# r's exponentials in place in PSUM, zero products in TensorE's first waits, casts behind the second pair's products, two weight quarters earlier, and two chunks' transposes on TensorE

## The chip, the cores and the metric

The kernel runs on one core of one Trainium2 chip. The metric is the device time of one execution in microseconds (us). Engines are named as in the profile: PE is TensorE's matmul, PEld its weight load, DVE is VectorE, ACT is ScalarE, POOL is GpSimd, SP is SyncE, which here issues nearly all DMAs.

## The reference

Two stages. The first is a linear attention with a decay per channel (4 batches, 8 heads, 768 positions, 48 channels per head), the second a feed-forward product with a leaky ReLU on its 3072 x 384 output:

```python
for t in range(S):
    cur = np.einsum('bhd,bhe->bhde', u[None] * kt, vt)
    y[:, :, t] = np.einsum('bhd,bhde->bhe', rt, state + cur)
    state = wt[:, :, :, None] * state + np.einsum('bhd,bhe->bhde', kt, vt)
x = y.transpose(0, 2, 1, 3).reshape(B * S, H * D)
h = x @ w_in                      # 384 -> 2048
out = np.maximum(0.01 * h, h) @ w_out   # 2048 -> 384
```

All inputs and the output are float32.

## The kernel before, in words

**Tiling.** The 3072 rows are 24 chunks of 128 positions, 6 for each batch. A chunk's attention gives y (128 x 384), which is transposed into columns of xT. Its feed-forward part is 4 up groups (12 matmuls each, xT by a quarter of w_in, line 821), a leaky ReLU by ACT (line 855), and 4 down groups (4 matmuls of 384 columns each, line 873) that add into one PSUM bank; the result is copied and stored. Chunks 0 and 1, and 2 and 3, are worked on together as a pair (`pair`, lines 491 to 666), the rest one by one (`single`, lines 668 to 794).

**Attention of a chunk.** ACT takes the logarithm of w into lw (line 332). PE sums it along the positions into the bank cp (`cum`, lines 521 and 691). The decay factors are exponentials of these sums (`grow`, line 342): er for r and ek for k. A single takes er from cp, and ek from ci = cp + lw, which DVE computes (line 716). A pair needs four: er[1] and ek[0] from cp, er[0] and ek[1] from two other sums, which for both pairs PE computes into two more banks (lines 543 and 544). DVE multiplies r by er and k by ek into rk (`product`, line 348). rk is transposed into rkT (`turn`): by four PE transposes for each of r and k (line 391), with copies out of PSUM by DVE (line 399) and ACT (line 401), or from chunk 12 on by one DMA transpose (line 382). Scores are products of rkT (lines 629 and 750), masked by DVE (line 412). The state goes from chunk to chunk: outer products of k and v (lines 594 and 761), added by DVE to the shrunken old state (line 434); POOL does the shrinking (line 421). y is the sum of products in bank yp (lines 646, 654, 780, 785) and of a diagonal term vs that POOL and DVE prepare (lines 357 to 371); DVE adds them (line 444). Then y is transposed by PE (line 458) and copied by ACT (line 465), from chunk 12 on by DMA (line 450). The a exponentials (lines 569 and 738) read cp as well.

**Order.** Nothing is ordered by hand. Each step is added to `Plan` with its engine, a cost in us and a priority; `Plan.order` runs a small model of the engines (line 71: PE costs count 1.8 times before 26 us of the model's time; lines 76 to 81: DMA) and the instructions are issued in the order of the model's start times. Each engine works through its instructions in that order. Attention of chunk n has priority 10n or 10n + 1 (smaller goes first), casts of the weights 3 (`CASTS`), feed-forward products 1000 and more. PE's instructions of all chunks are one queue, and so are DVE's and SP's.

**Weights.** w_in and w_out come as four quarters each (0.79 MB), loaded by SP (lines 290 and 295); each is cast to bf16, one half by DVE (line 313), the other by ACT (line 315). `WEIGHTS` says with which chunk a quarter is added and at which priority: the first with pair 2 at priority 20.15, the other seven with chunk 4 at 24. Pair 2's loads of w, k, r and v have 20.0, 20.1, 20.2 and 20.3, so the first quarter stands between k and r.

**PSUM.** Eight banks: hp and op two each, cp, yp, se and so one each. A `Ring` hands out its banks in turn; a step that writes a bank waits for all steps that used it before.

```python
PAIRS = (0, 2)
TDMA = range(12, NCH)
WEIGHTS = [(2, 20.15)] + [(4, 24.0)] * 7
CASTS = 3
```

Of the kernel before, what the change touches and what calls it, by code (L numbers as in the profile page):

```python
# [15 lines left out]
class Plan:  # L16
# [20 lines left out]
    def order(self):  # L37
# [19 lines left out]
        while events:  # L57
            now, e = heapq.heappop(events)
            if free[e] > now + 1e-9:
                continue  # L60
            while coming[e] and coming[e][0][0] <= now + 1e-9:
                _, i = heapq.heappop(coming[e])
                heapq.heappush(ready[e], (self.pri[i], i))
            if not ready[e]:
                if coming[e]:
                    heapq.heappush(events, (coming[e][0][0], e))
                continue
            _, i = heapq.heappop(ready[e])
            start[i] = now
            count += 1  # L70
            free[e] = now + self.dur[i] * (1.8 if e == "PE" and now < 26 else 1)
            if self.wire[i] is None:
                done[i] = free[e] + self.LAT[e]
            else:

                flying = [x for x in flying if x[0] > free[e]]
                while sum(x[1] for x in flying) + self.rows[i] > 3300:
                    free[e] = max(free[e], flying.pop(0)[0])
                dma_free = max(dma_free, free[e]) + self.wire[i]
                done[i] = dma_free + 1.6  # L80
                flying.append((done[i], self.rows[i]))
            heapq.heappush(events, (free[e], e))
            for j in users[i]:
                left[j] -= 1
                same = self.eng[j] == e and self.wire[i] is None
                ready_at[j] = max(ready_at[j], free[e] if same else done[i])
                if not left[j]:
                    f = self.eng[j]
                    heapq.heappush(coming[f], (ready_at[j], j))
                    heapq.heappush(events, (max(ready_at[j], free[f]), f))  # L90
# [33 lines left out]
def kernel(  # L124
# [23 lines left out]
    OACT = 14  # L148
    NCI = 3
    TDMA = range(12, NCH)  # L150
    LEAD = 8
    AHEAD = 5

    PAIRS = (0, 2)
    PWIRE, WIRE = 1.45, 1.15
    WEIGHTS = [(2, 20.15)] + [(4, 24.0)] * 7
    CASTS = 3
    blocks = [1] * NCH
# [9 lines left out]
    trev = pool.tile([128, 128], BF16, name="trev")  # L168
    trex = pool.tile([128, 128], BF16, name="trex")
    maskb = pool.tile([128, 128], BF16, name="maskb")  # L170
    pmask = pool.tile([128, 2, 128], BF16, name="pmask")
    pev = pool.tile([128, 128], BF16, name="pev")
    pex = pool.tile([128, 128], BF16, name="pex")
    halves = pool.tile([128, 2], BF16, name="halves")
    ident = pool.tile([128, 128], BF16, name="ident")
# [10 lines left out]
    ci_r = ring("ci", 2, [128, H, D], F32)  # L186
    er_r = ring("er", 3, [128, H, D], F32)
    ek_r = ring("ek", 2, [128, H, D], F32)
# [17 lines left out]
    cp_r = ring("cp", 1, [128, 512], F32, psum)  # L206
    yp_r = pp_r = ring("yp", 1, [128, 512], F32, psum)
    se_r = ring("se", 1, [128, 512], F32, psum)
    so_r = ring("so", 1, [128, 512], F32, psum)

    with tc.manual_schedule():
        nc.scalar.preload_act_table_set("natural_log_exp_and_others")

        for t, op in ((trev, ALU.is_ge), (trex, ALU.is_gt)):
            nc.gpsimd.memset(t[:], -1.0)
            nc.gpsimd.affine_select(
                out=t[:], in_=t[:], compare_op=op, fill=0.0,
                base=0, pattern=[[-1, 128]], channel_multiplier=1,
            )
# [21 lines left out]
        for q in (0, 64):  # L241
            for i, op in ((slice(0, 64), ALU.is_gt), (slice(64, 128), ALU.is_gt),
                          (slice(128, 192), ALU.is_ge), (slice(192, 256), ALU.is_gt)):
                t = pmask[q : q + 64].rearrange("p a t -> p (a t)")[:, i]
                nc.gpsimd.affine_select(
                    out=t, in_=t, compare_op=op, fill=0.0,
                    base=0, pattern=[[1, 64]], channel_multiplier=-1,
                )
        nc.vector.memset(onef[:], 1.0)
        nc.vector.memset(halves[:], 0.0)  # L250
# [34 lines left out]
        def weight_steps(q, which, pri):  # L285
# [13 lines left out]

            ld = step("SP", 0.45, load, pri, writes=[st], wire=2.0, rows=(384, 512)[which])  # L300
            made = []
# [42 lines left out]

        def product(rk, a, xn, e, P0, deps, n):
            return step(
                "DVE", 0.65 if n < 2 else 0.84 - 0.04 * a,
                lambda: nc.vector.tensor_tensor(out=rk.t[:, a, :, 0:D], in0=xn.t, in1=e.t[:], op=ALU.mult),  # L348
# [124 lines left out]
        def spread_u():  # L473
# [3 lines left out]
                -1, wire=0.05)  # L477
            up = op_r.take()
            s_ub = step(
# [11 lines left out]
        def pair(n):  # L491
# [45 lines left out]
            cums.extend([s_cum, s_cum])  # L537
            er = [er_r.take() for _ in range(2)]
            ek = [ek_r.take() for _ in range(2)]
            if n < NCI:  # L540
                cs = [(hp_r if n == 0 else op_r).take() for _ in range(2)]
                s_c = [
                    step("PE", 0.33, lambda: sums(cs[0].t, pev, pev), P0, reads=lw, writes=[cs[0]], deps=s_ln),
                    step("PE", 0.33, lambda: sums(cs[1].t, pex, pex), P0, reads=lw, writes=[cs[1]], deps=s_ln)]
                e_in = [hd(x.t[:, 0:DM]) for x in cs]
                s_w = []
            else:
                cs = [ci_r.take() for _ in range(2)]
                s_c = [
                    step(  # L550
                        "DVE", dve(DM, 120),
                        lambda j=j: nc.vector.tensor_tensor(
                            out=cs[j].t[:], in0=hd(cp.t[:, 0:DM]), in1=lw[j].t[:, :, 0:D],
                            op=(ALU.subtract, ALU.add)[j]),
                        P0, reads=[cp, lw[j]], writes=[cs[j]], deps=[s_cum])
                    for j in range(2)]
                e_in = [x.t[:] for x in cs]
                s_w = s_c
            mid = hd(cp.t[:, 0:DM])
            s_er1 = grow(er[1], cp, mid, 1.0, P0, [s_cum, *s_w])  # L560
            s_ek0 = grow(ek[0], cp, mid, -1.0, P0, [s_cum, *s_w])
            s_er0 = grow(er[0], cs[0], e_in[0], 1.0, P0, [s_c[0]])
            s_ek1 = grow(ek[1], cs[1], e_in[1], -1.0, P0, [s_c[1]])

# [12 lines left out]
            for j in range(2):  # L577
                s_k = product(rk[j], 1, kn[j], ek[j], P0, [kl, (s_ek0, s_ek1)[j]], n)
                s_r = product(rk[j], 0, rn[j], er[j], P0, [rl, (s_er0, s_er1)[j]], n)
                s_d.append([s_r, s_k])  # L580
# [5 lines left out]

            pps = [op_r.take(), op_r.take()] if n == 0 else [se_r.take(), so_r.take()]

# [79 lines left out]
        def single(n):  # L668
# [33 lines left out]
            cums.append(s_cum)  # L702
            er, ek = er_r.take(), ek_r.take()
            if n < NCI:
                cq = op_r.take()
                s_ci = step(
                    "PE", 0.17,
                    lambda: nc.tensor.matmul(
                        hd(cq.t[:, 0:DM]), lhsT=trex[:], rhs=lw.t[:, :, 0:D], start=True, stop=True),
                    P0, reads=[lw], writes=[cq], deps=[s_ln])  # L710
                ci, e_in, s_w = cq, hd(cq.t[:, 0:DM]), [s_cum]
            else:
                ci = ci_r.take()
                s_ci = step(
                    "DVE", dve(DM, 120),
                    lambda: nc.vector.tensor_tensor(  # L716
                        out=ci.t[:], in0=hd(cp.t[:, 0:DM]), in1=lw.t[:, :, 0:D], op=ALU.add),
                    P0, reads=[cp, lw], writes=[ci], deps=[s_cum, s_ln])
                e_in, s_w = ci.t[:], [s_cum, s_ci]
            s_er = grow(er, cp, hd(cp.t[:, 0:DM]), 1.0, P0, s_w)  # L720
            s_ek = grow(ek, ci, e_in, -1.0, P0, [s_ci])
            rk = rk_r.take()
            s_r = product(rk, 0, rn, er, P0, [rl, s_er], n)
            s_k = product(rk, 1, kn, ek, P0, [kl, s_ek], n)
            rkT = rkT_r.take()
# [7 lines left out]
            if not first:  # L733
# [5 lines left out]
                            out=a_in.t[q0 : q0 + 64, :, half], in_=cp.t[q0 : q0 + 64, DM : DM + NP], func=AF.Exp),  # L739
                        P0 + 1, reads=[cp], writes=[a_in], deps=s_w)  # L740
                    for half, q0 in ((0, 0), (1, 64))]
# [56 lines left out]
        while n < NCH:  # L798
# [3 lines left out]
            else:  # L802
                single(n)
                n += 1


# [90 lines left out]
        for n in range(NCH):  # L897
            if n >= LEAD:
                plan.deps[lns[n]].append(up_done[n - LEAD])
        for i in plan.order():  # L900
            plan.fn[i]()

# [29 lines left out]
```

## Time and profile before

| | us |
|---|---|
| median of 3 runs (lowest, highest) | 188.97 (188.82, 189.43) |
| the profiled execution | 188.97 |
| its span from first to last instruction | 187.3 |
| PE busy | 174.0 (93%) |
| DVE busy | 128.0 (68%) |
| ACT busy | 116.3 (62%) |
| POOL busy | 108.7 (58%) |
| first up group | 19.84 |
| last down group begins / copy of the last result | 180.44 / 183.90 |

The profile is one execution. Busy times are sums over an engine's instructions; matmuls are pipelined, so 12 matmuls that each take 0.219 us fill 0.67 us when they follow one another. In a line of the order in time the first figure is the start, the second the time covered, then engine, line of the kernel, operation, output<-input by the program's names, shape and count; in brackets how long the engine was idle before it and what released it. A group's line has busy us, mean ns of one, and the idle time before. The chain that ended last is followed back from the last instruction. "issue" is a wait for nothing that the profile shows.

### The profile page before, as it was taken

The page shows a single profiled execution, that of the slowest core. Times are in us where ns is not written, and L with a number is a line of the kernel's source. Part 1 is how long each engine was busy: PE and PEld are TensorE (multiplying, and loading weights), DVE is VectorE, ACT ScalarE, POOL GpSimd, SP SyncE. Part 2 cuts the span into 40 slices and gives each one's busy share as a digit, 9 for nine tenths or more (in the row PEclk, how much of TensorE's full clock was granted, in tenths as well). Part 3 has the DMA queues.
Part 4 walks back from the last instruction along what each step waited for, and adds up shares of the span by engine and source line. Part 5 has one row for each costly group of instructions (what it writes and reads, how often), then busy time and mean ns, then how long its engine had stood idle before and what let it go on. Part 6 is the DMA issues. An engine that isn't in the chain of part 4 may idle for free.

```text
span 187.3 us, 6219 instructions
## 1 busy us (share of the span) xinstructions
PE 174.0 (93%) x2550; PEld 136.1 (73%) x2550; DVE 128.0 (68%) x226; ACT 116.3 (62%) x254; POOL 108.7 (58%) x148
## 2 busy tenths in 40 slices
PE   3678579999999999999999999999999999999992
PEld 1255567688778878788787787878887877877871
DVE  2399784887789787877967999766876856441111
ACT  2646586678876877796687666676374645334430
POOL 7799922175899898978792885170545755400000
PEclk9999999999999999999999999999999999999999
DMA  5999999889899997987899879997789996512102
GB/s 147 261 316 322 385 370 302 156 189 217 164 221 211 185 221 158 221 193 172 174 207 190 156 155 229 119 200 141 159 180 179 191 202 142 123 44 67 38 7 84
DMA packets 116383, 34.62 MB, mean 185 GB/s; under 512 B 109697, under 2 KB 114818, under 8 KB 116354
## 3 DMA queue, kind: packets, MB, share of 16 engines
q1 hardware_dynamic: 116352, 34.22, 82.9%
q8 instruction: 20, 0.33, 0.7%
q14 instruction: 9, 0.07, 0.1%
q10 hardware_dynamic: 2, 0.00, 0.0%
HBM read 25.17 MB, written 4.72 MB: 160 GB/s over the span
## 4 chain that ended last, share of the span: by engine, by line
PE 81%; SPq 7%; DMA 6%; issue 1%; POOL 1%; DVE 1%; POOLq 0%; DVEq 0%
PE op L873 33%; PE hp L821 32%; DMA in<-in_moe_w_out_dram 6%; SPq L470 4%; PE se L750 3%; SPq L290 3%; PE yp L785 2%; PE cp L691 2%; PE yp L761 2%; PE yp L780 1%; PE so L391 1%; PE se L391 1%; PE yp L458 1%; PE cp L696 1%; PE yp L654 1%
## 5 line engine op out<-in xcount | busy, mean ns | idle before, releaser
L855 ACT ACTIVATE g<-hp 128x512 bf16<-128x512 f32 x96 | 57.1, 597 | 42.3 <-PE hp L821 41.4
L821 PE MATMUL hp<-xT,w_in_b 128*128 128x128 bf16 x1152 | 79.0, 219 | 0.3 <-DVE rkT L399 0.3
L873 PE MATMUL op<-w_out_b,g 128*128 128x384 bf16 x384 | 76.5, 326 | 0.8 <-DVE w_out_b L313 0.8
L821 PEld LDWEIGHTS <-w_in_b 128*128 128x128 bf16 x1152 | 69.3, 98 | 7.2 <-DVE w_in_b L313 0.2
L873 PEld LDWEIGHTS <-g 128*128 128x128 bf16 x384 | 33.0, 97 | 15.6 <-issue 0.9
L357 POOL TENSOR_TENSOR ru<-in,ub 128x384 f32<-128x384 f32 x24 | 26.9, 1119 | 19.7 <-DMA in<-in_r_dram 19.7
L369 POOL TENSOR_TENSOR vs<-in,dg 128x384 f32<-128x384 f32 x24 | 20.2, 843 | 14.7 <-DVE dg L365 11.0
L361 POOL TENSOR_TENSOR ru<-ru,in 128x384 f32<-128x384 f32 x24 | 25.7, 1072 | 0.9
L348 DVE TENSOR_TENSOR rk<-in,er 128x384 bf16<-128x384 f32 x24 | 18.2, 757 | 7.4 <-DMA in<-in_r_dram 5.5
L348 DVE TENSOR_TENSOR rk<-in,ek 128x384 bf16<-128x384 f32 x24 | 22.0, 919 | 1.4 <-ACT a L738 0.9
L421 POOL TENSOR_TENSOR sb<-s,a 128x384 bf16<-128x384 f32 x17 | 16.1, 947 | 10.7 <-DVE s L434 10.1
L412 DVE TENSOR_TENSOR m<-se,maskb 128x512 bf16<-128x512 f32 x20 | 13.8, 689 | 7.3 <-PE so L750 7.1
L444 DVE TENSOR_TENSOR y<-yp,vs 128x384 bf16<-128x384 f32 x24 | 13.3, 553 | 7.5 <-PE yp L785 5.1
L889 DVE COPY o<-op 128x384 f32<-128x384 f32 x10 | 5.6, 558 | 18.2 <-PE op L873 18.1
L337 POOL CAST vb<-in 128x384 bf16<-128x384 f32 x24 | 14.6, 614 | 4.5 <-DMA in<-in_v_dram 4.5
L332 ACT ACTIVATE lw<-in 128x384 bf16<-128x384 f32 x24 | 12.4, 520 | 3.9 <-DMA in<-in_w_dram 3.8
L365 DVE TENSOR_REDUCE dg<-ru 128x8 f32<-128x384 f32 x24 | 13.0, 543 | 1.9 <-POOL ru L361 1.8
L412 DVE TENSOR_TENSOR m<-so,maskb 128x512 bf16<-128x512 f32 x20 | 13.6, 680 | 0.0
L342 ACT ACTIVATE er<-cp 128x384 f32<-128x384 f32 x22 | 10.8, 492 | 3.5 <-DVE ci L716 3.0
L716 DVE TENSOR_TENSOR ci<-cp,lw 128x384 f32<-128x384 f32 x20 | 11.0, 549 | 1.8 <-ACT g L855 0.9
L342 ACT ACTIVATE ek<-ci 128x384 f32<-128x384 f32 x20 | 10.5, 526 | 0.0
L391 PEld LDWEIGHTS <-rk 128*128 128x128 bf16 x96 | 6.7, 103 | 5.0 <-DVE rk L348 4.2
(103 smaller groups left out, 191.0 us busy)
## 6 DMA issues: line engine op xcount, KB each, us to landing
out_dram<-o SPq DMA_DIRECT2D x24, 192.0 KB, 2.5
in<-in_w_dram SPq DMA_DIRECT2D x20, 192.0 KB, 3.6
in<-in_k_dram SPq DMA_DIRECT2D x20, 192.0 KB, 3.8
in<-in_r_dram SPq DMA_DIRECT2D x20, 192.0 KB, 3.9
in<-in_v_dram SPq DMA_DIRECT2D x20, 192.0 KB, 3.8
in<-in_moe_w_in_dram SPq DMA_DIRECT2D x4, 768.0 KB, 8.5
in<-in_moe_w_out_dram SPq DMA_DIRECT2D x4, 768.0 KB, 12.6
in<-in_w_dram SPq DMA_DIRECT2D x2, 384.0 KB, 5.0
```

Of the source, the lines that this page charges most:

```text
L337: "POOL", 0.57, lambda: nc.gpsimd.tensor_copy(out=vb.t[:], in_=vn.t),
L342: "ACT", 0.5, lambda: nc.scalar.activation(out=out.t[:], in_=i, func=AF.Exp, scale=scale),
L348: lambda: nc.vector.tensor_tensor(out=rk.t[:, a, :, 0:D], in0=xn.t, in1=e.t[:], op=ALU.mult),
L357: lambda: nc.gpsimd.tensor_tensor(out=ru.t[:], in0=rn.t, in1=ubv, op=ALU.mult),
L361: lambda: nc.gpsimd.tensor_tensor(out=ru.t[:], in0=ru.t[:], in1=kn.t, op=ALU.mult),
L369: lambda: nc.gpsimd.tensor_tensor(out=vs.t[:], in0=vn.t, in1=dg.t[:].unsqueeze(2).to_broadcast([128, H, D]), op=ALU.mult),
L412: lambda par=par: nc.vector.tensor_tensor(out=m.t[:, par], in0=gt(sc[par].t), in1=mask.unsqueeze(1).to_broadcast([128, NP, 128]), op=ALU.m ...
L421: lambda: nc.gpsimd.tensor_tensor(out=sb.t[:].rearrange("p g a d -> p (g a) d"), in0=s_in.t[:].rearrange("p g a d -> p (g a) d"), in1=a_ap ...
L444: lambda: nc.vector.tensor_tensor(out=y.t[:], in0=hd(yp.t[:, 0:DM]), in1=vs.t[:], op=ALU.add),
L821: nc.tensor.matmul(hp.t[:, a * N : (a + 1) * N], lhsT=w_in_b[:, t, (j + a) * 128 : (j + a + 1) * 128], rhs=xT[:, t, c0 : c0 + N], start=(a ...
L855: lambda hp=hp, g=g, j=j, J=J, N=N: nc.scalar.activation(out=g.t[:, j : j + J, 0:N], in_=hp.t[:, 0 : J * N].rearrange("p (a n) -> p a n", ...
L873: nc.tensor.matmul(op.t[:, 0:DM], lhsT=g.t[:, j, off : off + 128], rhs=w_out_b[:, j, :], start=(j == 0), stop=(j == NJ - 1))
```

## The change

Six things are different:

1. The exponentials er for r are written over the sums that they are made from: into cp, and for er[0] of a pair into the bank of its own sum. The buffers er are gone. ek[1] of a pair is written in place as well (a PSUM bank for pair 0, the SBUF buffer ci for pair 2). Where er and ek both come from cp, ek is computed first.
2. Pair 2 computes its second extra sum on DVE (cp + lw) and no longer on PE.
3. As long as the previous PE step ends before 24 us of the model's time, each PE step is preceded by products of a tile of zeros (256 columns each, into the second op bank): one per 0.13 us of 70% of the gap that the model leaves between the two steps. The first op bank alone (`pre_r`) serves the steps that took op banks before; pair 0's second outer product goes to the yp bank.
4. Casts of the weights have priority 21 in place of 3.
5. Two weight quarters are loaded at priority 4, behind pair 0's loads and ahead of pair 2's; the other six at 24, behind pair 2's.
6. DMA transposes begin with chunk 14, not 12. The model's constants are others: the factor 1.8 ends at 6 us and not at 26, DMA times are a few per cent longer, products count 0.58 or 0.84.

```diff
-            free[e] = now + self.dur[i] * (1.8 if e == "PE" and now < 26 else 1)
+            free[e] = now + self.dur[i] * (1.8 if e == "PE" and now < 6 else 1)
...
-    TDMA = range(12, NCH)
+    TDMA = range(14, NCH)
...
-    PWIRE, WIRE = 1.45, 1.15
-    WEIGHTS = [(2, 20.15)] + [(4, 24.0)] * 7
-    CASTS = 3
+    PWIRE, WIRE = 1.5, 1.18
+    WEIGHTS = [(2, 4.0)] * 2 + [(4, 24.0)] * 6
+    WARM = 24.0
+    CASTS = 21
...
+    pre_r = Ring(op_r.tiles[:1])
...
-            er = [er_r.take() for _ in range(2)]
-            ek = [ek_r.take() for _ in range(2)]
-            if n < NCI:
-                cs = [(hp_r if n == 0 else op_r).take() for _ in range(2)]
+            for j, banks in enumerate((hp_r, hp_r) if n == 0 else (pre_r, None)):
...
+            mid = View(cp, hd(cp.t[:, 0:DM]))
+            ek = [ek_r.take(), e_in[1]]
+            er = [e_in[0], mid]
+            s_ek0 = grow(ek[0], cp, mid.t, -1.0, P0, [s_cum, *s_w])
+            s_er1 = grow(mid, cp, mid.t, 1.0, P0, [s_cum, s_ek0, *s_w])
+            s_er0 = grow(er[0], cs[0], er[0].t[:], 1.0, P0, [s_c[0]])
+            s_ek1 = grow(ek[1], cs[1], ek[1].t[:], -1.0, P0, [s_c[1]])
...
-            pps = [op_r.take(), op_r.take()] if n == 0 else [se_r.take(), so_r.take()]
+            pps = [pre_r.take(), yp_r.take()] if n == 0 else [se_r.take(), so_r.take()]
...
+            er = View(cp, hd(cp.t[:, 0:DM]))
+            s_er = grow(er, cp, er.t, 1.0, P0, [s_cum, s_ci])
+            s_ek = grow(ek, ci, ci.t[:], -1.0, P0, [s_ci])
...
+        at = 0.8
         for i in plan.order():
+            if plan.eng[i] == "PE" and at < WARM:
+                for _ in range(int((plan.start[i] - at) * 0.7 / 0.13)):
+                    nc.tensor.matmul(
+                        op_r.tiles[1][:, 0:256], lhsT=zeros[:, 0:128], rhs=zeros[:], start=True, stop=True)
+                at = plan.start[i] + plan.dur[i]
             plan.fn[i]()
```

## The prediction

> **What bounds the kernel now.** I read the busy times by stage first, then the order in time from 4 to 50 us, then the chain that ended last, then the groups. By stage (stage, its length, busy us and instructions of each engine, granted clock, DMA share, GB/s):
>
> ```profile
> 20.00:25.00 5.00, 2.78 (x48) 2.44 (x44) 5.00 (x7) 3.92 (x7) 2.99 (x3) 1.00 1.05 376
> 25.00:30.00 5.00, 3.95 (x65) 3.24 (x63) 3.70 (x8) 4.03 (x7) 1.75 (x3) 1.00 1.07 373
> 30.00:35.00 5.00, 5.00 (x99) 3.50 (x98) 2.79 (x5) 3.93 (x8) 0.73 (x1) 1.00 0.97 215
> ...
> 40.00:60.00 20.00, 20.00 (x306) 16.54 (x304) 16.44 (x29) 15.74 (x35) 15.70 (x19) 1.00 0.92 194
> ...
> 180.00:187.30 7.30, 3.86 (x31) 2.31 (x28) 1.12 (x2) 0.60 (x1) 0.00 (x0) 1.00 0.14 54
> ```
>
> From 30 us to the last product PE (first figure) has no gap; the chain agrees, 81% of it is PE. So the end is fixed by two things: how much work PE has, and how much of it is behind PE when it becomes saturated. Nothing on VectorE, ScalarE or DMA after some 50 us counts unless it starves PE. Before 30 us PE waits; in 20 to 25 us VectorE is busy all 5.00 us and DMA is full. What PE waits for:
>
> ```profile
> 19.84 0.83 PE L821 MATMUL hp<-xT,w_in_b 128*128 128x128 bf16 x12
> ...
> 22.73 0.34 PE L458 MATMUL yp<-ident,y 128*128 128x128 bf16 x3 [2.06 <-DVE y L444]
> ...
> 27.31 0.81 PE L873 MATMUL op<-w_out_b,g 128*128 128x384 bf16 x4 [0.79 <-DVE w_out_b L313]
> ```
>
> VectorE is late with chunk 1's y, because these stood in its queue: w_in casts of 1.21 and 1.02 us and a product of 1.08 us. The weights arrive so:
>
> ```profile
> 14.14 0.83 ACT L315 CAST w_in_b<-in 128x768 bf16<-128x768 f32 x1 [0.89 <-DMA in<-in_moe_w_in_dram]
> ...
> 19.99 0.83 ACT L315 CAST w_in_b<-in 128x768 bf16<-128x768 f32 x1 [1.31 <-DMA in<-in_moe_w_in_dram]
> ...
> 24.08 0.83 ACT L315 CAST w_in_b<-in 128x768 bf16<-128x768 f32 x1 [0.36 <-DMA in<-in_moe_w_in_dram]
> ...
> 26.40 0.83 ACT L315 CAST w_out_b<-in 128x768 bf16<-128x768 f32 x1 [0.51 <-DMA in<-in_moe_w_out_dram]
> ```
>
> One quarter per 2.1 us; the last w_out quarter is cast at 32.88. Chunk 2's columns of xT come only at 37.37, chunk 4's at 49.55:
>
> ```profile
> 36.89 0.48 ACT L465 COPY xT<-yp 128x384 bf16<-128x384 bf16 x1 [1.49 <-PE yp L458]
> ```
> ```profile
> 49.09 0.46 ACT L465 COPY xT<-yp 128x384 bf16<-128x384 bf16 x1
> ```
>
> So between 20 and 37 us PE has only chunks 0 and 1: 8 groups of up products (12 matmuls, 0.667 us) and 8 of down products (4, 0.65).
>
> **Part by part.** *Transposes of chunks 12 and 13 back on PE.* 22 transposes. The four at 24.13 take 0.40 us, one lasts 0.228, so they start (0.40 - 0.228)/3 = 0.057 us apart; the twelve of a group give 0.667/12 = 0.056. 22 x 0.056 = **+1.23 us** on a saturated PE, nothing hides it. The copies out of PSUM (2 x 0.42 on VectorE, 2 x (0.59 + 0.48) on ScalarE) lie beside PE; both are under 85% busy there. The four DMA transposes leave a queue nobody on the path waits for: 0.
>
> [...]
>
> *Pair 2's pex sum moves from PE to VectorE.* Two matmuls of 384 columns (4 in 0.65 us): **-0.33 us** on PE; +0.55 on VectorE (ci row below).
>
> *Exponentials in place.*
>
> ```profile
> L348 DVE TENSOR_TENSOR rk<-in,ek 128x384 bf16<-128x384 f32 x24 | 22.0, 919 | 1.4 <-ACT a L738 0.9
> ...
> L444 DVE TENSOR_TENSOR y<-yp,vs 128x384 bf16<-128x384 f32 x24 | 13.3, 553 | 7.5 <-PE yp L785 5.1
> ...
> L342 ACT ACTIVATE er<-cp 128x384 f32<-128x384 f32 x22 | 10.8, 492 | 3.5 <-DVE ci L716 3.0
> ```
>
> No row shows an exponential written to PSUM, nor a product read from it. For the product, bounds are 0.54 (r's product at 23.54 to 24.55, with POOL idle) and 1.08 (at 21.13, with POOL busy); I take 0.55, the y row, the same shape with one operand in PSUM, which stays at 0.553 whatever POOL does. Mean now 0.757: 24 x 0.2 = 4.9 us off VectorE, off the path except in the first 30 us. For the write I take 0.49, bounds 0.45 and double; double would be 12 us more on a ScalarE that is 62% busy, and about 1 us in each early chain. The new wait: cp, one bank, is held until r's product has read it, and the next chunk's cum stands in PE's queue with all products behind it. But cp is already held by the a exponentials (38.99 to 39.33 for chunk 4, its r product ended at 39.03), so it comes free no later: 0.
>
> *Zero products.* They sit in PE's queue before steps that are planned later. A planned gap gets 0.7/0.13 of them per us. Early matmuls are slow:
>
> ```profile
> 5.15 0.48 PE L521 MATMUL cp<-lw,pex 128*128 128x384 bf16 x1 [1.29 <-ACT lw L332]
> ...
> 5.56 0.48 PE L521 MATMUL cp<-lw,pev 128*128 128x384 bf16 x1
> ```
>
> 384 columns per 0.41 us, against 0.163 in the chain's rows, while the granted clock reads 1.00 throughout. 256 columns then cost 0.27 us and overfill the gap by 45%; at the later pace 0.11 and they fill 59%. Of the first two gaps (some 12 and 9 products) I expect cum 0 to 2 us later than 5.15, say 1.4, and the following steps at the fast pace. r lands at 7.67 anyway, three of pair 0's four products take 0.55 in place of up to 1.3, so the products end near 10 instead of 11.5.
>
> [...] My sum books nothing for the pace itself.
>
> *Two weight quarters behind pair 0's loads, six behind pair 2's.* SP's order was: pair 0 (w, k, r, v), pair 2's w, k, quarter 0, r, v, seven quarters. Pair loads come some 1.55 us apart (quarter 0 at 14.14, r at 15.69). New order from v at about 9.1: quarters at 11.2 and 13.3 (were 14.14, 19.99), w 14.9 (was at most 10.68), k 16.4, r 18.0 (was 15.69), v 19.5, the rest as before. So up products of both quarters can run as soon as xT is there.
>
> *Casts at priority 21* stand behind pair 2's products, evacuations and masks. In 17 to 33 us VectorE loses 0.68 + 1.21 + 1.02 + 0.68 + 0.85 + 0.56 + 0.56 us of casts from the front of its queue; they run in its waits instead. Price: each cast may come some 0.3 us later.
>
> *Sum.* Chunk 0 and 1 reach xT near 17 and 19.5 (18.7 and 23.7), so all 8 up groups are done at 26, one cast after quarter 3. Pair 2: products end near 21 (24.55), then the chain to xT, 12.8 us now, loses 2.65 us of casts: 31 instead of 37.4. PE's work at 30 us, before: 6 up groups, 1.2 down, pair 2 through its outer products. After: 8 up, 2.5 down, and pair 2 with both scores and one y (0.4 + 0.4 + 0.65, less the 0.33 that is gone). That is 1.33 + 0.85 + 1.15 = 3.3 us further. PE then has down groups until 31, and chunk 2 follows. -3.3 + 1.23 - 0.33 = -2.4 us; for waits where PE's fixed order meets other times than the model's I add 0.4. **-2.0 us** on the profiled execution's 188.97 (span 187.3 and 1.67 around it), which is also the median of the runs: **187.0 us**.
>
> **Rivals.** *Chunk 4 starves PE.* Being 3.3 us ahead, PE runs out of chunks 0 to 3 near 48 us. Chunk 4's loads keep their place behind all weights; r came at 36.55, xT at 49.55. If that stays, 1.1 to 1.6 us are lost again: 188.3. Against it: of those 13 us, several are VectorE's queue and slow products. *Pair 2 late, slower.* r comes 2.3 us later and w 4.3. Chunks 0 and 1 give PE work until about 34.4 only; for each us that chunk 2's xT comes after that, PE idles. With the 0.9 us of added work the change breaks even when xT of chunk 2 lands at about 36.6; if the chain from r does not shrink but for 1 us, it lands at 38.5, and the time is 190.5. For it: the delay is certain. Against it: VectorE held pair 2's products for 8.9 us after r had come. *The early part does nothing*: fillers and slow writes to PSUM give back what the shorter products bring, PE is only 1 us further at 30 us, and the 0.9 us of added work cancels it: 188.9.
>
> **Numbers.** Forecast 0.55; chunk 4 starves 0.17 (0.10 of it faster, 0.07 same); pair 2 late 0.20 (0.17 slower, 0.03 same); early part does nothing 0.08 (0.05 same, 0.03 slower). A measurement of this kernel can tell about 0.3% (0.57 us) from no change: faster 0.65, same 0.15, slower 0.20. The range goes down to 185.6 (no added waits, and one and a half more down groups, 1.0 us, done at 30 us) and up to 189.8, which takes in the unknown prices and a part of the late pair.
>
> **What would show it.** First up group near 17 us; all eight of chunks 0 and 1 by 26.5; chunk 2's xT copy near 31 (beyond 36.6 I am wrong in sign); no PE gap at 45 to 50; r's product at 0.55; cum near 6.5; casts of w_in after pair 2's products on VectorE; 22 more transposes at 0.056.

## The result and the profile after

The changed kernel takes **190.4 us** (median of 6 runs, 189.83 to 190.71) against 188.9 for the kernel before (188.65 to 189.43, 6 runs): ratio 1.007 (95%: 1.0049 to 1.0092), slower by 0.7%. The prediction said 187.0, in 185.6 to 189.8; the sign was wrong. Ratios here and below leave out runs over 1.5% above their kernel's fastest (one took 255.83 us); medians take in all. The profiled execution's span is 188.6 us, before 187.3.

By stage, the changed kernel (columns as in the prediction: length, busy us and instructions of PE, PEld, DVE, ACT, POOL, granted clock, DMA share, GB/s):

```profile
20.00:25.00 5.00, 4.30 (x66) 3.40 (x65) 3.64 (x7) 3.20 (x6) 4.92 (x6) 1.00 1.01 341
25.00:30.00 5.00, 3.13 (x71) 2.77 (x72) 4.48 (x9) 3.43 (x6) 3.16 (x4) 1.00 1.07 382
30.00:35.00 5.00, 4.74 (x112) 3.71 (x111) 3.22 (x6) 3.49 (x6) 0.00 (x0) 1.00 0.89 231
...
40.00:60.00 20.00, 20.00 (x284) 16.11 (x282) 13.65 (x25) 15.91 (x37) 14.30 (x18) 1.00 0.85 183
180.00:188.60 8.60, 5.16 (x47) 3.35 (x44) 1.11 (x2) 1.19 (x2) 0.00 (x0) 0.99 0.12 46
```

PE is busier than before at 20 to 25 us (4.30 for 2.78), much of it zero products, and idler at 25 to 30 (3.13 for 3.95) and 30 to 35 (4.74 for 5.00). From 40 us it has no gap, as before. So the frame of the prediction stands: the end is PE's work plus what PE lost before it became saturated. The two can be counted from the PE records (each useful matmul at its spacing in a stream: 0.056 us for 128 columns and 0.163 for 384 in the traces, that is 0.417 ns a column plus 2.5 ns, and the same line for other widths; the smallest ones of attention at their own spacing; zero products left out). What the smallest ones are booked at is a choice, so the rows are an estimate; up to 30 us the differences between the columns are good to some 0.4 us.

| PE, us | before | after |
|---|---|---|
| useful work in all | 162.50 | 163.40 |
| time without useful work up to 40 us | 16.78 | 17.42 |
| useful work done at 25 us | 9.50 | 10.08 |
| useful work done at 30 us | 13.22 | 12.97 |
| up / down groups done at 30 us | 6.0 / 1.2 | 6.0 / 0.8 |
| up / down groups done at 35 us | 8.0 / 5.0 | 8.0 / 3.5 |

At 40 us the changed kernel has lost 0.64 us more than the one before; by 180 us 0.42 of it is left. 0.90 of work (1.23 - 0.33) and 0.42 of lost time make the 1.3 us of the span. The prediction had the work right; it expected the work done at 30 us to be 3.3 us more, and it is some 0.3 less. PE's order in time in the changed kernel shows where the time goes:

```profile
18.95 0.84 PE L815 MATMUL hp<-xT,w_in_b 128*128 128x128 bf16 x12
...
20.63 0.83 PE L815 MATMUL hp<-xT,w_in_b 128*128 128x128 bf16 x12
...
22.68 0.71 PE L899 MATMUL op<-zeros 128*128 128x256 bf16 x5
...
24.14 0.84 PE L815 MATMUL hp<-xT,w_in_b 128*128 128x128 bf16 x12
26.24 1.51 PE L815 MATMUL hp<-xT,w_in_b 128*128 128x128 bf16 x24 [1.26 <-DVE w_in_b L314]
```

The groups at 18.95, 20.63 and 24.14 are chunk 0's, by the first three quarters. The pair at 26.24 is chunk 0's fourth and chunk 1's first. Chunk 1's columns of xT were there at 22.47 and the first quarter since 12.04, yet its first group stands in PE's queue behind chunk 0's fourth, which waits for the fourth quarter.

This wait is not of the same length in every execution. In a second profile of the changed kernel it is 0.96 us. The first experiment below has the same instructions in the same order up to 90 us; in its profile the fourth quarter's cast begins 0.95 us earlier, and the third and fourth group of chunk 0 and the first of chunk 1 run without a pause (that execution was the shortest of its 12, 188.26 us):

```profile
24.34 2.47 PE L815 MATMUL hp<-xT,w_in_b 128*128 128x128 bf16 x36
```

VectorE's queue in the changed kernel, in the same stretch:

```profile
23.23 0.40 DVE L400 COPY rkT<-se 128x512 bf16<-128x512 bf16 x1
25.49 0.69 DVE L314 CAST w_in_b<-in 128x768 bf16<-128x768 f32 x1 [1.86 <-DMA in<-in_moe_w_in_dram]
26.10 0.54 DVE L435 TENSOR_TENSOR s<-se,sb 128x384 f32<-128x384 f32 x1
```

The same fourth quarter holds VectorE for 1.86 us with pair 2's state addition behind it, though the outer products that it adds were done at 24.21. ACT's casts, copies into xT and one leaky ReLU:

```profile
11.21 0.83 ACT L316 CAST w_in_b<-in 128x768 bf16<-128x768 f32 x1 [0.81 <-DMA in<-in_moe_w_in_dram]
13.31 0.83 ACT L316 CAST w_in_b<-in 128x768 bf16<-128x768 f32 x1 [1.27 <-DMA in<-in_moe_w_in_dram]
...
17.53 0.48 ACT L466 COPY xT<-yp 128x384 bf16<-128x384 bf16 x1
...
22.00 0.47 ACT L466 COPY xT<-yp 128x384 bf16<-128x384 bf16 x1
...
25.49 0.83 ACT L316 CAST w_in_b<-in 128x768 bf16<-128x768 f32 x1 [1.80 <-DMA in<-in_moe_w_in_dram]
26.23 0.59 ACT L849 ACTIVATE g<-hp 128x512 bf16<-128x512 f32 x1
...
34.72 0.47 ACT L466 COPY xT<-yp 128x384 bf16<-128x384 bf16 x1
```

Quarters 1 and 2 come at the predicted times. The fourth is cast at 25.49 (before 24.08), the last at 33.98 (32.88). Chunk 0's xT ends at 18.01 (17 predicted, 18.68 before), chunk 1's at 22.47 (19.5 predicted, 23.72 before), chunk 2's at 35.19 (31 predicted, 37.37 before). The leaky ReLU at 26.23 is that of chunk 0's third group, which PE had finished at 24.98; it stood behind the cast that waited 1.80 us, and chunk 1's first group needs the bank that it frees.

What did happen as predicted: r's product from PSUM, and the exponential in place (groups of the changed kernel: busy us, mean ns of one | idle before):

```profile
L349 DVE TENSOR_TENSOR rk<-in,cp 128x384 bf16<-128x384 f32 x22 | 12.1, 549 | 3.8 <-ACT cp L343 3.5
...
L343 ACT ACTIVATE cp<-cp 128x384 f32<-128x384 f32 x22 | 10.7, 488 | 1.3 <-DVE ci L707 1.3
```

and the start, where cum comes at 5.91 (6.5 predicted, 5.15 before) and in this profile runs at the fast pace at once:

```profile
4.81 1.27 PE L899 MATMUL op<-zeros 128*128 128x256 bf16 x10
5.91 0.33 PE L522 MATMUL cp<-lw,pex 128*128 128x384 bf16 x1
6.08 0.33 PE L522 MATMUL cp<-lw,pev 128*128 128x384 bf16 x1
```

Two products of 384 columns start 0.17 us apart, where before they were 0.41 apart. In the second profile of the changed kernel cum comes at 7.47 and they are 0.32 apart: the moment at which PE becomes fast differs from one execution to the next (last section).

### The profile page after: what moved, and what is told of

The parts are those of the page before. It is cut to its first block, busy times and chain, and to the rows that moved or that the text cites. A ratio compares the mean times of both kernels' runs of the same rounds, so it can differ in the third digit from the quotient of the medians.

```text
span 188.6 us, 6389 instructions
## 1 busy us (share of the span) xinstructions
PE 179.1 (95%) x2639; PEld 142.2 (75%) x2639; DVE 119.3 (63%) x230; ACT 118.6 (63%) x258; POOL 101.7 (54%) x146
## 4 chain that ended last, share of the span: by engine, by line
PE 83%; SPq 9%; DMA 5%; ACT 1%; issue 1%; DVE 0%
PE op L867 34%; PE hp L815 33%; SPq L471 6%; DMA in<-in_moe_w_out_dram 5%; PE se L742 3%; SPq L291 3%; PE yp L777 2%; PE cp L692 2%; PE yp L753 2%; PE yp L772 2%; PE so L392 1%; PE se L392 1%; PE yp L459 1%; PE cp L697 1%; PE yp L655 1%
## 5 line engine op out<-in xcount | busy, mean ns | idle before, releaser
L358 POOL TENSOR_TENSOR ru<-in,ub 128x384 f32<-128x384 f32 x24 | 23.9, 997 | 14.2 <-DMA in<-in_r_dram 12.7
L422 POOL TENSOR_TENSOR sb<-s,a 128x384 bf16<-128x384 f32 x17 | 15.2, 892 | 23.2 <-DVE s L435 10.9
L362 POOL TENSOR_TENSOR ru<-ru,in 128x384 f32<-128x384 f32 x24 | 24.6, 1027 | 0.8
L445 DVE TENSOR_TENSOR y<-yp,vs 128x384 bf16<-128x384 f32 x24 | 13.4, 557 | 13.3 <-PE yp L777 9.0
L349 DVE TENSOR_TENSOR rk<-in,ek 128x384 bf16<-128x384 f32 x22 | 15.3, 697 | 6.7 <-ACT ek L343 6.5
L338 POOL CAST vb<-in 128x384 bf16<-128x384 f32 x24 | 13.2, 552 | 3.2 <-DMA in<-in_v_dram 2.0
L349 DVE TENSOR_TENSOR rk<-in,cp 128x384 bf16<-128x384 f32 x22 | 12.1, 549 | 3.8 <-ACT cp L343 3.5
L899 PE MATMUL op<-zeros 128*128 128x256 bf16 x69 | 10.8, 298 | 1.1 <-DVE zeros L249 1.1
L343 ACT ACTIVATE cp<-cp 128x384 f32<-128x384 f32 x22 | 10.7, 488 | 1.3 <-DVE ci L707 1.3
L435 DVE TENSOR_TENSOR s<-yp,sb 128x384 f32<-128x384 f32 x14 | 7.8, 556 | 5.5 <-PE yp L753 3.5
```

Of the source, the lines that this page charges most:

```text
L338: "POOL", 0.57, lambda: nc.gpsimd.tensor_copy(out=vb.t[:], in_=vn.t),
L358: lambda: nc.gpsimd.tensor_tensor(out=ru.t[:], in0=rn.t, in1=ubv, op=ALU.mult),
L362: lambda: nc.gpsimd.tensor_tensor(out=ru.t[:], in0=ru.t[:], in1=kn.t, op=ALU.mult),
L422: lambda: nc.gpsimd.tensor_tensor(out=sb.t[:].rearrange("p g a d -> p (g a) d"), in0=s_in.t[:].rearrange("p g a d -> p (g a) d"), in1=a_ap ...
L445: lambda: nc.vector.tensor_tensor(out=y.t[:], in0=hd(yp.t[:, 0:DM]), in1=vs.t[:], op=ALU.add),
```

## The experiments

Ratios are to the kernel before, run in turn with each on the same chip, with 95% intervals. 0.1% is 0.19 us.

**Parts of the change undone, one at a time.** The theory after the result: the loss has three terms, the transposes, the weight order and the zero products. The rival: the attention of chunk 2 is still late because of VectorE's queue, and the weights' order has no part in it.

*The transposes*, in the changed kernel:

```diff
-    TDMA = range(14, NCH)
+    TDMA = range(12, NCH)
```

> The changed kernel with one part undone: chunks 12 and 13 are transposed by DMA again. Theory A (PE is saturated after 35 us, so its 22 transposes cost 22 x 0.056 = 1.23 us, and the rest of the loss is made before 30 us): 1.0 to 1.3 us less than the changed kernel, some 189.2, 0.2 to 0.5 above the kernel before. Rival (the DMA transposes were no gain, because PE had room there or because the queue is relieved): within 0.3 of the changed kernel, 190.1 to 190.7.

Measured: 0.998 (0.9952 to 1.0007), 189.11 us. *The same two chunks put on PE in the kernel before* (`range(14, NCH)` there):

> The kernel before, with DMA transposes from chunk 14 on and nothing else: the cost of 22 PE transposes by itself. Prediction and theory A: 1.0 to 1.4 us above the kernel before. Rival (DMA transposes cost PE waits that come back): within 0.5 us of it.

Measured: 1.0076 (1.005 to 1.0101), 190.69 us. So the 22 transposes cost some 1.4 us, in either kernel (0.9 to 1.9 by the second interval), against 1.23 predicted; that term is right within the noise. They alone are as large as the whole loss.

*The weight order:*

```diff
-    WEIGHTS = [(2, 4.0)] * 2 + [(4, 24.0)] * 6
+    WEIGHTS = [(2, 20.15)] + [(4, 24.0)] * 7
```

> The changed kernel with the weight quarters where they were: the first between pair 2's k and r, seven behind pair 2. Theory A (the two early quarters bring nothing, since chunk 1's up products stand behind chunk 0's fourth, and the quarters behind pair 2 come 1.2 us later): the third quarter's cast back near 22.0 and the fourth's near 24.1, and 0.4 to 1.0 us less than the changed kernel, some 189.7. Rival (the early quarters help as predicted and something else eats it): 0.5 us or more above the changed kernel.

Measured: 0.9983 (0.9961 to 1.0004), 189.05 us. The last cast goes back to 32.91, chunk 2's xT comes at 34.17 (35.19), and up to 40 us PE is 16.08 us without useful work (17.42): 1.34 us, the size of the gain. In this order of the program the early quarters cost time instead of bringing it.

*The zero products:*

```diff
-    WARM = 24.0
+    WARM = 0.0
```

> The changed kernel without any product of zeros; the order of all other instructions is the same. Theory A (the fillers lie in waits that PE has anyhow): within 0.5 of the changed kernel, or up to 1 us more, since the first steps are slow again. Rival B (7.5 us of zero products stand in PE's queue ahead of real steps and push pair 0 and pair 2 back): at least 0.6 less, 189.8 or below.

Measured: 1.0025 (1.0004 to 1.0045), 189.86 us; against 1.007 and 1.0056 for the whole change the products cost 0.6 to 0.85 us here.

*The casts' priority:*

```diff
-    CASTS = 21
+    CASTS = 3
```

> The changed kernel with the casts at priority 3, ahead of pair 2's steps, as before. Theory A (the casts stand in VectorE's queue by the model's landing times, whatever their priority): within 0.4 of the changed kernel. Rival C (priority 21 makes the weights late): 0.6 us or more below it, the fourth quarter of w_in cast earlier than 25.49.

Measured: 1.0011 (0.9982 to 1.004), 189.6 us, chunk 2's xT at 36.72. Chunk 2 comes 1.5 us later and the kernel is not slower but 0.8 to 1.1 us faster, while chunk 1's second and third up groups are done at 30.1 instead of 31.1 and PE has no gap from 30 to 35 us. So in the changed kernel it was not chunk 2's arrival that decided.

**Parts together.** The whole change once more, and combinations:

> The changed kernel itself, unaltered, beside the next three on one chip, since the four undone parts gave 0.9 to 1.7 us each by ratios from different chips, which is more than the whole loss. If those sizes are real: ratio to the kernel before 1.007 again (1.3 us). If they came from the chip: 1.002 to 1.004.

Measured: 1.0056 (1.0036 to 1.0077), 190.43 us, as the first time.

Old weight order and old transposes together:

```diff
-    TDMA = range(14, NCH)
+    TDMA = range(12, NCH)
...
-    WEIGHTS = [(2, 4.0)] * 2 + [(4, 24.0)] * 6
+    WEIGHTS = [(2, 20.15)] + [(4, 24.0)] * 7
```

> The changed kernel with two parts undone: the weight quarters in their old place and chunks 12 and 13 transposed by DMA. What stays is the exponentials in place, the zero products and the casts at 21. Theory A (parts add up): 1.0 to 1.3 us below the kernel with the old weight order alone, which was 0.3 us below the kernel before: 1.2 to 1.6 us below the kernel before, ratio 0.992 to 0.994. Rival (every undone part gives the same 0.9 us, because the changed kernel sits on one unlucky order that any edit breaks): ratio 0.997 to 1.000.

Measured: 0.9935 (0.9909 to 0.9961), 188.17 us. The two losses add up, and what is left of the change beats the kernel before by 0.65%.

The same without zero products (`WARM = 0.0`):

> As the kernel with the two parts undone, and no zero products. If they are in the way (the changed kernel got 0.85 us faster without them, by ratios): 0.5 us or more below that kernel. If they only fill waits: within 0.4 us of it, or above it.

Measured: 0.9946 (0.9914 to 0.9977), 188.59 us; its runs lie between 187.28 and 189.47, those of the last kernel between 187.91 and 188.25. In this order the zero products cost nothing that can be told.

And with the casts in front as well (`CASTS = 3`), which leaves the exponentials in place, pair 2's second sum on VectorE, the bank changes and the model's constants:

> Of the change, only the exponentials in place (with pair 2's second sum on VectorE and the model's new constants) stay: old weight order, casts at 3, DMA transposes from chunk 12, no zero products. Theory A: VectorE's products give most of the gain of the early part: 0.5 to 1.3 us below the kernel before. Rival (pair 2 gains nothing from shorter products, since its chain waits for other things): within 0.4 us of the kernel before.

Measured: 1.0157 (1.0116 to 1.0198), 192.55 us. This is the change's rival "pair 2 late" in pure form. VectorE's order in time in that kernel:

```profile
26.54 0.56 DVE L314 CAST w_out_b<-in 128x768 bf16<-128x768 f32 x1
28.63 0.56 DVE L314 CAST w_out_b<-in 128x768 bf16<-128x768 f32 x1 [1.53 <-DMA in<-in_moe_w_out_dram]
30.74 0.56 DVE L314 CAST w_out_b<-in 128x768 bf16<-128x768 f32 x1 [1.55 <-DMA in<-in_moe_w_out_dram]
32.89 0.74 DVE L314 CAST w_out_b<-in 128x768 bf16<-128x768 f32 x1 [1.59 <-DMA in<-in_moe_w_out_dram]
33.55 0.54 DVE L435 TENSOR_TENSOR s<-se,sb 128x384 f32<-128x384 f32 x1
```

Four casts, three of which wait for their DMA, stand ahead of pair 2's state addition, which runs at 33.55. In the kernel with the casts at 21 it runs at 24.97:

```profile
23.76 1.27 DVE L314 CAST w_in_b<-in 128x768 bf16<-128x768 f32 x2
24.97 0.56 DVE L435 TENSOR_TENSOR s<-se,sb 128x384 f32<-128x384 f32 x1
```

So chunk 2's xT comes at 40.57 instead of 34.12, and PE has no up or down group between 35.1 and 40.6 us. The span is 4.1 us longer (4.0 by the two ratios).

**The weight order's cause.** Theory: the early quarters can't be used, since hp has two banks that go round in the program's order, all four groups of chunk 0 first. Then two groups of chunk 1, by the two early quarters, put behind chunk 0's first two should turn the loss into a gain. Rival: the quarters' later arrival is the loss, and the order of the groups matters little. In the changed kernel, ahead of the loop that hands out the feed-forward groups:

```diff
+        early = [s for s in seq if s[0] == 0 and s[1] == 1][:2]
+        seq = [s for s in seq if s not in early]
+        seq[2:2] = early
```

> The changed kernel, but chunk 1's first two up groups stand between chunk 0's second and third in the order of the feed-forward products, so that hp banks come to them before the third and fourth quarter are cast. Theory A (the early quarters bring nothing because the two hp banks go round in a fixed order, chunk 0's four groups first): 5 up groups done at 25 us in place of 3, and 0.5 to 1.3 us less than the changed kernel, 189.1 to 189.9. Rival (PE's work at 30 us is held by pair 2's chain on VectorE and POOL, and the groups only change places): within 0.4 of the changed kernel.

Measured: 0.996 (0.9937 to 0.9984), 188.75 us, 1.7 us less than the whole change without it. PE's order in time in that kernel:

```profile
22.97 1.50 PE L815 MATMUL hp<-xT,w_in_b 128*128 128x128 bf16 x24
...
24.85 0.84 PE L815 MATMUL hp<-xT,w_in_b 128*128 128x128 bf16 x12
26.18 1.51 PE L815 MATMUL hp<-xT,w_in_b 128*128 128x128 bf16 x24 [0.49 <-DVE w_in_b L314]
...
28.74 0.81 PE L870 MATMUL op<-w_out_b,g 128*128 128x384 bf16 x4 [1.04 <-DVE w_out_b L314]
```

Chunk 1's two groups run at 22.97, where zero products and a pause were. The quarters land as late as in the changed kernel (the fourth is cast at 25.43) and chunk 2's xT is hardly earlier (35.10), so the rival falls: it is the order of the groups. The next wait, at 28.74, is for the first quarter of w_out; that part of the later arrival remains. Against the old weight order (0.9983) this kernel is not clearly faster: the intervals overlap. The move takes away what the early quarters cost; a gain by them can't be told. The same move with the old weight order was not run, so how much of the 1.7 us it would bring without early quarters is open.

The other wait, VectorE's 1.86 us: the model takes the fourth quarter to have landed when it has not. With the model's landing later by 1.5 us:

```diff
-                done[i] = dma_free + 1.7
+                done[i] = dma_free + 1.7 + (1.5 if self.pri[i] == 24.0 else 0)
```

> The changed kernel, ordered by a model in which the six late quarters land 1.5 us later, as they do in the trace. Theory A2 (casts stand in VectorE's queue ahead of pair 2's state and masks and hold them, because the model takes the quarters for landed): VectorE's wait before the fourth w_in cast (1.86 us) is gone, and 0.4 to 1.0 us less than the changed kernel. Rival (the quarters' landing itself is the bound): within 0.3 of it.

Measured: 1.0034 (1.002 to 1.0049), 189.8 us. Its VectorE in order of time:

```profile
25.37 0.55 DVE L366 TENSOR_REDUCE dg<-ru 128x8 f32<-128x384 f32 x1 [1.38 <-POOL ru L362]
25.84 0.83 DVE L314 CAST w_in_b<-in 128x768 bf16<-128x768 f32 x1
26.59 0.53 DVE L435 TENSOR_TENSOR s<-se,sb 128x384 f32<-128x384 f32 x1
```

The wait for DMA is gone, and a wait of 1.38 for POOL has taken its place: the state addition is at 26.59 and was at 26.10. Yet the kernel is 0.4 to 0.7 us faster than the changed one (1.0056 and 1.007), so the gain did not come by pair 2's state. PE's order in time shows another way:

```profile
25.43 0.83 PE L815 MATMUL hp<-xT,w_in_b 128*128 128x128 bf16 x12 [0.24 <-ACT g L849]
26.73 1.51 PE L815 MATMUL hp<-xT,w_in_b 128*128 128x128 bf16 x24 [0.46 <-DVE w_in_b L314]
```

The group at 25.43 ends before VectorE's cast of the fourth quarter does (26.67), so it is chunk 1's first, now ahead of chunk 0's fourth, and it begins when ACT has freed its bank. The banks alone thus did not put it behind: the model did, which took the fourth quarter to be there. Later landings in the model moved one group, the experiment before it two.

**What the casts are worth outside the change.** `CASTS = 21` in the kernel before, alone:

> The kernel before, with the casts at priority 21 and nothing else. If the casts' place alone brings what the old weight order, casts at 21 and exponentials in place brought together (1.2 us below the kernel before): 0.8 to 1.5 us below it. If the exponentials in place are needed for it: within 0.4 us of the kernel before, or above.

Measured: 1.0054 (1.0022 to 1.0086), 190.81 us: slower, while beside the exponentials in place, with old weights and old transposes, the same edit is worth 4 us (1.0157 against 0.9946), and in the whole change it costs 0.8 to 1.1. Is it the model's constants that make the difference? The kernel before with the change's constants (1.8 until 6 us, the DMA times) and, in both, all transposes on PE:

```diff
-            free[e] = now + self.dur[i] * (1.8 if e == "PE" and now < 26 else 1)
+            free[e] = now + self.dur[i] * (1.8 if e == "PE" and now < 6 else 1)
...
-    TDMA = range(12, NCH)
+    TDMA = range(NCH, NCH)
...
-    PWIRE, WIRE = 1.45, 1.15
+    PWIRE, WIRE = 1.5, 1.18
```

> The kernel before with the model's new constants (factor 1.8 up to 6 us, landings 0.1 us later, transfers 0.03 to 0.1 us longer) and PE transposes in all chunks, casts at 3. PE transposes of twelve more chunks come after 100 us and cost 12 x 0.614 = 7.4 us; what is read is the first 50 us and the difference to the next kernel. If constants and casts decide together: chunk 2's xT beyond 38 us and 2 to 4 us above the next kernel. If only the exponentials in place made the kernel with casts at 3 slow (1.0157): within 1 us of the next kernel.

Measured: 1.0392 (1.033 to 1.0454), 196.23 us; chunk 2's xT at 37.63. With `CASTS = 21`:

> As the kernel with new constants and PE transposes in all chunks, with casts at 21. If the order alone carries the gain of the early part: chunk 2's xT near 34, and the time 7.4 - 1.2 = 6.2 us above the kernel before (ratio near 1.033). If an added instruction is needed for it: 7.4 us or more above (1.039 and up).

Measured: 1.0449 (1.0407 to 1.049), 197.61 us; xT at 35.84, earlier, yet PE is 18.08 us without useful work up to 40 us, against 16.39. Part of that is PE's pace, which becomes fast at 28.04 us in this profile and at 23.69 in the other; the intervals of the two ratios overlap. So constants and priority together show no gain either. Which other piece does (pair 2's second sum on VectorE, ek in place, the bank changes, the products' costs in the model) stays open.

**What the exponentials in place are worth.** The best version so far (old weights, old transposes) with r's exponentials in a ring of three SBUF buffers again:

```diff
+    er_r = ring("er", 3, [128, H, D], F32)
...
-            er = View(cp, hd(cp.t[:, 0:DM]))
-            s_er = grow(er, cp, er.t, 1.0, P0, [s_cum, s_ci])
+            er = er_r.take()
+            s_er = grow(er, cp, hd(cp.t[:, 0:DM]), 1.0, P0, [s_cum, s_ci])
```

> The changed kernel with old weight order and DMA transposes from chunk 12 (ratio 0.9935), but r's exponentials written to SBUF as before; the model's costs are not altered. If their place in PSUM is what the gain needs (VectorE's products 0.2 us and more shorter in the first 30 us): 0.6 us or more above that kernel, r's products at 0.7 or more. If the order alone does it: within 0.4 us of that kernel.

Measured: 0.9924 (0.9897 to 0.9952), 188.32 us: no difference from 0.9935 that can be told. The groups with SBUF buffers:

```profile
L350 DVE TENSOR_TENSOR rk<-in,ek 128x384 bf16<-128x384 f32 x22 | 18.6, 844 | 7.9 <-ACT ek L344 7.7
L350 DVE TENSOR_TENSOR rk<-in,er 128x384 bf16<-128x384 f32 x24 | 19.3, 806 | 4.1 <-ACT er L344 4.0
```

and in PSUM, same kernel otherwise:

```profile
L349 DVE TENSOR_TENSOR rk<-in,ek 128x384 bf16<-128x384 f32 x22 | 15.7, 713 | 8.0 <-ACT ek L343 7.3
...
L349 DVE TENSOR_TENSOR rk<-in,cp 128x384 bf16<-128x384 f32 x22 | 12.1, 548 | 4.0 <-ACT cp L343 3.9
```

Each r product is 0.26 us shorter, k's 0.13: some 9 us off VectorE, and nothing that can be told off the time. So VectorE's work after 40 us is not what bounds the kernel.

**A better version.** The interleaved groups with the old transposes (`TDMA = range(12, NCH)`):

> The changed kernel with chunk 1's first two up groups ahead of chunk 0's third, and chunks 12 and 13 transposed by DMA. If the parts add: 1.0 to 1.4 us below the same kernel with PE transposes (ratio 0.996 to the kernel before), so ratio 0.988 to 0.991, 186.9 to 187.5. If the gains overlap: not below the old weight order with DMA transposes, 0.9935.

Measured: 0.992 (0.9895 to 0.9944), 188.09 us. With the later landing in the model:

> As the kernel with interleaved up groups and DMA transposes, ordered by a model in which the six late quarters land 1.5 us later. In the changed kernel this gave 0.4 to 0.6 us. If the two cures are for different waits: 0.3 us or more below that kernel. If both cure the same wait of PE at 25 us: within 0.3 of it.

Measured: 0.9915 (0.9893 to 0.9938), 187.99 us: the same. Without zero products:

> As the kernel with interleaved up groups and DMA transposes, without zero products. With the early quarters the changed kernel gained 0.6 to 0.85 us without them, with the old order nothing. If the fillers stand in the way of the early steps: 0.3 us or more below. If they only fill waits and give the early steps their pace: within 0.3, or above.

Measured: **0.990 (0.9872 to 0.9927), 187.8 us**, the lowest ratio of all, 1.0% below the kernel before; its interval overlaps those of the two before it and of the two kernels with old weights and DMA transposes (0.9935 and 0.9924), so which of these is best is not shown.

## Why the prediction was wrong

Point by point, by the prediction's own steps:

- *Transposes +1.23 on a saturated PE*: right within the noise. 1.4 us measured alone (ratio 1.0076, 0.9 to 1.9 us), 0.90 together with the pex sum in PE's records. That is 1.4 / 22 = 0.064 us each.
- *pex sum -0.33*: right within the 0.90.
- *Exponentials in place: 0.55 and 0.49, cp held no longer*: right, 0.549 and 0.488; that the shorter products lie off the path is right as well (0.9924 against 0.9935).
- *Zero products book nothing; cum near 6.5*: cum came at 5.91 in one profile and at 7.47 in the other. That they cost nothing was mis-sized: 0.6 to 0.85 us in the changed order, none that can be told in the other two. What they stand in the way of is open. The reading that the granted clock was 1.00 while the products were slow does not hold: the trace has no clock record before 17.71 us (last section).
- *Quarters at 11.2 and 13.3*: exact. *"the rest as before"*: wrong by 1.1 to 1.4 us in the profile of the changed kernel (the last cast at 33.98, before 32.88). By 17.5 us more bytes had come than before (4.60 MB, before 4.44), by 25 us fewer (6.95, before 7.30). Why is not settled, and it is not the same in every execution: with the same order of loads the last cast came at 33.03 in the profile of the first experiment.
- *r at 18.0, pair 2's products end near 21*: 18.93 and 22.08; right within 1.1 us.
- *"all 8 up groups are done at 26"*: **this is the step that failed**, and with it the 3.3 us that PE was to be ahead at 30. 3 were done at 26 us and 6 at 30. The prediction let a group run "as soon as xT is there" and its quarter; it did not ask in which order the groups stand in PE's queue. Chunk 1's first group stood behind chunk 0's fourth and could not have its bank before chunk 0's third was through ACT, so the early quarters served one group at a time and PE waited for the fourth. Moving two groups forward brought 1.7 us at once. It did not bring the forecast: with the move 5 groups were done at 26 us, 7.2 at 30, and PE's work at 30 us was some 0.6 us ahead of the kernel before, not 3.3.
- *"Chunk 0 and 1 reach xT near 17 and 19.5"*: 18.01 and 22.47. Of the three pieces that were to stand in VectorE's queue ahead of chunk 1's y, the cast of 1.02 us starts at 22.60 and stands behind it, so there was less to gain. With xT at 22.47 and the fourth quarter cast at 26.32, eight groups by 26 were out of reach in any order.
- *"the chain to xT loses 2.65 us of casts: 31"*: failed as well. The chain from the last product takes 35.19 - 22.08 = 13.1 us, before 12.8. The casts left the front of the queue, but one of them, with its wait, was put ahead of the state addition, and where it was moved POOL's ru took its place.
- *Break-even at 36.6 for chunk 2's xT*: the rule presumed that chunks 0 and 1 keep PE busy until chunk 2 is due. Where they nearly did (exponentials in place, casts at 3, old weights) it held: that kernel has 0.33 us less work in place of 0.90 more, which moves the balance to 36.6 + 0.90 + 0.33 = 37.8, and an xT at 40.57 should cost 2.7 us against the kernel before. Its ratio gives 3.0 (2.2 to 3.7). In the changed kernel PE lost its time earlier, the most of it at 24.98 to 26.24, and an xT at 35.19 was no help.
- *Rivals*: "pair 2 late" gave the number (190.5) but not the mechanism, since chunk 2 came before 36.6. What happened is nearest to "the early part does nothing" (188.9), with a loss on top. "Chunk 4 starves PE" did not occur: no gap at 45 to 50.

The loss is thus accounted for in the main: the transposes (some 1.4 us) and the early quarters in this order (0.85 to 1.6 us, from the ratios with and without them), against the 0.65% (1.2 us) by which the rest of the change beats the kernel before when these two are undone. The zero products' 0.6 to 0.85 us shows only beside the early quarters and is no third addend. Not settled: why the later quarters slip, what the zero products stand in the way of, and which piece of the change makes the casts' priority pay.

## What to carry to other kernels

Data that comes earlier helps only if the work that uses it stands next in its engine's queue (here 1.7 us lay in the place of two groups): before booking a gain, write out the queue's order, the banks' rotation included, and ask what each instruction ahead of it waits for. A step that waits for a DMA (1.86 us on VectorE here) belongs behind everything that is ready, and removing it showed the next wait (1.38 us for POOL), not the end of waiting. Work added to an engine that is saturated to the end counted in full here, at its spacing in a stream (1.23 us booked, some 1.4 measured), and was the term that held. And one profile is one execution: the same instructions lost some 0.8 us less of PE's time up to 40 us in one profile (that of the first experiment) than in two others, so a difference of that size needs the ratio of the runs beside it.

## What the runs showed of the hardware

- PE had two paces, and the clock's column does not show when the second began. The trace's clock records begin at 17.71 us in the kernel before, with 1.00; the column counts the time without a record as 1.00 too, so what the clock was in that time is not shown. Up to that moment products of 128 columns start 0.107 us apart in a stream, after it 0.056; the four transposes at 8.28 us take 0.61 us, those at 24.13 take 0.40. In the changed kernel without zero products the record begins at 24.82, and the up groups on either side of it show the two paces:

```profile
20.41 1.46 PE L815 MATMUL hp<-xT,w_in_b 128*128 128x128 bf16 x12
22.52 1.49 PE L815 MATMUL hp<-xT,w_in_b 128*128 128x128 bf16 x12
26.04 2.36 PE L815 MATMUL hp<-xT,w_in_b 128*128 128x128 bf16 x36
```

- Products of zeros brought that moment forward here: it lies between 3.84 and 10.15 us in the eleven profiles with them and between 17.71 and 28.04 in the nine without, and it differs between profiles of the same kernel (4.19 and 9.92 in the changed one). The time did not gain by it: without them the changed kernel was 0.6 to 0.85 us faster.
- With the exponentials in place alone the clock fell again: the record says 0.5 from 37.98 to 41.40 us, and the same product took 0.32 us before and 0.50 in it. PE was busy 3.65 us of the 5.00 from 35 to 40; that this made the clock fall is not shown:

```profile
35.00:40.00 5.00, 3.65 (x118) 2.76 (x117) 4.56 (x8) 1.92 (x7) 3.20 (x4) 0.80 1.03 240
```
```profile
35.48 0.32 PE L692 MATMUL cp<-lw,trev 128*128 128x384 bf16 x1 [0.34 <-ACT lw L333]
...
39.00 0.50 PE L692 MATMUL cp<-lw,trev 128*128 128x384 bf16 x1
```

- A VectorE product with one operand in PSUM took 0.54 to 0.56 us each time in the changed kernel (22 products of r, mean 0.549; the 15 that POOL was busy beside from start to end 0.542 to 0.555, the 3 with POOL idle the same); with both in SBUF single ones took 0.54 to 1.36 (in the kernel before 0.548 to 1.355 in the 20 with POOL busy throughout, 0.536 to 0.559 in the 8 with POOL idle), with means from 0.66 to 0.92 in the kernels here. k's mean fell from 0.844 to 0.713 between the two kernels above, but that is not shown to be r's doing: in the interleaved kernel, with r's exponentials in PSUM, it is 0.847.
- Writing an exponential over its own PSUM input costs ACT 0.488 us, as much as writing it to SBUF (0.492).
